# Two 64-column matmuls in place of one 128-column matmul, in the fp32 part of a linear-attention and mixer kernel

## The chip, the cores and the metric

One Trainium2 chip, one of its cores. The metric is device microseconds of one execution of the whole program. Of the kernel before there are three timed runs: 1278.36, 1279.97 and 1280.24 us, median 1279.97 us. One more execution was recorded by the hardware profiler.

## The reference

Random-feature attention over 8 batches, 8 heads, 576 tokens of 64 dimensions, then a token mixer and a two-layer MLP on the result. Cut to what matters:

```
phi(x): proj = x @ w_phi;  proj -= max|proj|;  return [exp(proj), exp(-proj)]      # 64 -> 2*128 features
kv  = phi(k).T @ v                  # per head 256 x 64, and z = sum of phi(k) over the tokens
out = phi(q) @ kv / (phi(q) @ z + 1e-6)
x   = heads side by side            # 8 x 576 x 512
u   = x + (x.T @ U @ V).T           # U 576 x 32, V 32 x 576
y   = u + relu(u @ w_ch1) @ w_ch2   # 512 -> 2048 -> 512
```

## The kernel before, in words

The work goes by **pairs** of heads: 8 batches with 4 pairs each. `Pair` loads k, q and v, transposes k and q on TensorE (`transposes`, L268), projects them with `w_phi` (`project_k`, `project_q`), makes the features (`k_features`, `q_features`; the maximum for q is a reduction over partitions on GpSimd, L327), and then has two steps that the change touches:

- *features with v*: `kv_tail` (L392) and `kv_main` (L400) add up `kv_ps`, 128 features x (64 values and one column of ones) for each half `f` of the 256 features and each of the two heads. The stationary operand is a 128 x 128 block of features (tokens x features), the moving one 65 columns of `vb`, or for the 64 left-over tokens of both heads ("tail") 130 columns of `vt`. `kv_done` (L407) copies the sum out of PSUM.
- *features with that product*: `out_tail` (L423) and `out_main` (L437) take 128 x 128 blocks of the q features as the stationary operand and 65 (tail: 130) columns of `kv` as the moving one. `normalize` divides.

All operands of these four are fp32. The program has one matmul for each; the hardware executes each fp32 one as two weight loads (LDWEIGHTS) and two matmuls, so that the profile counts 1024 for L403, where the program has 512, and as many for L442. Most other matmuls (the MLP at L559 and L576) use fp32r operands and are one load and one matmul each.

After the last pair of a batch, `Tokens` applies U and V (`down` L504, `up` L520) and the `Mixer` runs the MLP: `transposes` (L542) brings four token tiles into `uT_hi` and `uT_lo`, `hidden` (L553, 12 matmuls of 128x512) and `add` (L569, 12 more) run 16 times per batch. These MLP pieces are put into a list, and a hand-written loop (L724 to L757) calls a few of them between the steps of the next batch's pairs, so that TensorE has work while other engines make features. A ninth Mixer group holds the left-over tokens of all batches and runs last; its transposes stand at about 1170 us. In the first batch there is no MLP work yet; dummy matmuls (`keep_busy`, L655) fill some of the gaps.

What each engine does in which order is settled when the program is built: a scheduler with a timing model of its own orders the instructions of each engine by expected times, and each engine then runs its list strictly in that order. PSUM has three pools of banks: `at` (3 banks), `ph` (1), `o` (4). The last four hold the sum of the MLP's second layer from the first `add` of a batch to `finish` (L588), where VectorE adds them to `st`.

Of the kernel before, what the change touches and what calls it, by code (L numbers as in the profile page):

```python
# [18 lines left out]
PSUM = bass.MemoryType.PSUM  # L19
DRAM = bass.MemoryType.DRAM  # L20
P = 128


@with_exitstack
def tile_kernel(
# [12 lines left out]
    nc = tc.nc  # L38
    B, H, S, D = q.shape
    F = w_phi.shape[1]  # L40
# [5 lines left out]
        a.bitcast(I32).rearrange("a (b w) -> a b w", w=2) for a in (U, V, w1, w2))  # L46
    NT = S // P
    SM = NT * P
    ST = S - SM
    NPAIR = H // 2  # L50
    NCC = C // P
    NFC = DFF // P
    assert D == 64 and F == P and ST == 64 and 4 * R == P and B % 2 == 0

# [13 lines left out]
    def ps(name, tag="at"):  # L68
        return psum.tile([P, 512], F32, tag=tag, bufs=BANKS[tag], name=name)

# [158 lines left out]
    class Pair:  # L229
# [162 lines left out]
        def kv_tail(self):  # L392
            self.kv_ps = self.ps("kv_ps", True)
            self.kv_v = self.kv_ps[:, 0:4 * (D + 1)].rearrange("p (f h e) -> p f h e", f=2, h=2)
            for f in range(2):
                nc.tensor.matmul(  # L396
                    self.kv_v[:, f, :, :], self.kpt[:, 0, f * F:(f + 1) * F], self.vt,
                    start=(f == 0), stop=False, skip_group_check=True)

        def kv_main(self, g, kp):  # L400
            for t in range(NT):
                for f in range(2):
                    nc.tensor.matmul(  # L403
                        self.kv_v[:, f, g, :], kp[:, t, f * F:(f + 1) * F], self.vb[:, g, t, :],
                        start=False, stop=(t == NT - 1), skip_group_check=True)

        def kv_done(self):  # L407
            self.kv = small.tile([P, 2, 2, D + 1], F32, tag="kv", bufs=1, name=f"kv{self.nm}")
# [14 lines left out]
        def out_tail(self, xt):  # L423


            xp = self.ps("xpt", True)
            xv = xp[:, 0:2 * (D + 1)].rearrange("p (g e) -> p g e", e=D + 1)
            for f in range(2):
                nc.tensor.matmul(  # L429
                    xv, self.qpt[:, f, :], self.kv[:, f, :, :], start=(f == 0), stop=(f == 1))  # L430
            for g in range(2):
                rows = slice(g * ST, (g + 1) * ST)
                self.normalize(
                    f"t{g}", xv[rows, g:g + 1, :],
                    xt[self.tail, (self.h0 + g) * D:(self.h0 + g + 1) * D].unsqueeze(1), rows)

        def out_main(self, s, qp, x):  # L437
            xp = self.ps(f"xp{s}_", True)
            xv = xp[:, 0:NT * (D + 1)].rearrange("p (c e) -> p c e", e=D + 1)
            for c in range(NT):  # L440
                for f in range(2):
                    nc.tensor.matmul(  # L442
                        xv[:, c, :], qp[:, f, c * P:(c + 1) * P], self.kv[:, f, c // 2, :],
                        start=(f == 0), stop=(f == 1))
            xo = x.rearrange("p (z s) c -> p s z c", s=2)[:, s, :, self.h0 * D:(self.h0 + 2) * D]
            self.normalize(s, xv, xo.rearrange("p z (g d) -> p g z d", g=2))

# [350 lines left out]
```

## Time and profile before

| what | value |
|---|---|
| timed runs, median (lowest to highest) | 1279.97 us (1278.36 to 1280.24) |
| the profiled execution: span from first to last instruction | 1276.3 us |
| what lies around that span, if this execution took the median | 3.7 us |
| granted TensorE clock, mean | 0.994 |
| TensorE matmuls | 6976, busy 1244.0 us (97%) |
| TensorE weight loads | 6976, busy 1062.4 us (83%) |
| VectorE / ScalarE / GpSimd busy | 674.4 / 546.9 / 206.2 us |

The profile gives the execution's span and no other time of its own, so the third row is the difference to the median of the timed runs. In a profile, PE stands for TensorE's matmuls and PEld for its weight loads, which run beside them; DVE is VectorE, ACT ScalarE, POOL GpSimd. A row of a timeline is: start in us, length in us, engine, line of the kernel, operation, output<-inputs, size of the stationary operand (128\*128), output size, count. The length of a matmul there includes the time in the pipe and overlaps the next; what a matmul costs in a stream is the distance from its start to the next start.

### The profile page before, as it was taken

How to read it: one execution, taken by the hardware profiler on the slowest of the kernel's cores; microseconds unless marked ns; L12 is line 12 of the kernel's file. 1: busy time of each engine (PE TensorE's matmuls, PEld its weight loads, DVE VectorE, ACT ScalarE, POOL GpSimd, SP SyncE). 2: the span in 40 equal slices, each digit the busy share in tenths (PEclk: the TensorE clock that was granted, in tenths of full speed). 3: DMA queues.
4: the chain of work that ended last, by engine and by line, in shares of the span. 5: the costliest groups of instructions: out<-in, count | busy, mean ns of one | idle time of the engine just before them, and what ended most of it. 6: DMA issues, size and time to landing. Idle time of an engine off the chain costs nothing.

```text
span 1276.3 us, 18436 instructions
## 1 busy us (share of the span) xinstructions
PE 1244.0 (97%) x6976; PEld 1062.4 (83%) x6976; DVE 674.4 (53%) x1597; ACT 546.9 (43%) x1230; POOL 206.2 (16%) x184
## 2 busy tenths in 40 slices
PE   8999898999999999999999999999999999999997
PEld 6878677788888888888888888888888888788886
DVE  6579999755456455455545545545545542211211
ACT  6578777644443444344443444344434431111110
POOL 3335443301111111111110111011111110000000
PEclk9999998999999999999999999999999999999999
DMA  4245343421112111211112012211122002100001
GB/s 120 66 132 152 109 126 111 116 93 25 36 57 79 29 28 54 79 57 28 54 40 86 21 29 70 80 29 29 53 71 65 26 1 79 66 1 1 34 1 33
DMA packets 95159, 75.41 MB, mean 59 GB/s; under 512 B 52320, under 2 KB 77280, under 8 KB 94944
## 3 DMA queue, kind: packets, MB, share of 16 engines
q1 hardware_dynamic: 95072, 74.25, 19.4%
q8 instruction: 55, 0.90, 0.3%
q14 instruction: 32, 0.26, 0.1%
HBM read 55.35 MB, written 18.87 MB: 58 GB/s over the span
## 4 chain that ended last, share of the span: by engine, by line
PE 84%; DVE 11%; DMA 2%; ACT 1%; issue 1%; SPq 1%; POOL 0%; DVEq 0%; POOLq 0%
PE o L576 28%; PE ph L559 28%; PE xp L442 8%; PE kv_ps L403 7%; DVE w L141 2%; PE T L283 2%; PE pk L363 2%; DVE w_ab L149 1%; PE pp L514 1%; DMA w<-in_moe_w_ch_dram 1%; PE pt L546 1%; PE pq L386 1%; PE kv_ps L396 1%; PE xpt L429 1%; DVE w_ab L146 1%; PE pq L387 1%
## 5 line engine op out<-in xcount | busy, mean ns | idle before, releaser
L576 PE MATMUL o<-w_hi,h_hi 128*128 128x512 f32 x576 | 231.6, 404 | 1.3 <-ACT h_hi L564 0.9
L559 PE MATMUL ph<-uT_hi,w_hi 128*128 128x512 f32 x576 | 227.8, 396 | 1.8 <-ACT uT_hi L223 1.3
L559 PE MATMUL ph<-uT_lo,w_hi 128*128 128x512 f32 x576 | 227.8, 395 | 0.8 <-DVE uT_lo L224 0.8
L565 DVE SCALAR_TENSOR_TENSOR h_lo<-ph,h_hi 128x512 fp32r<-128x512 f32 x144 | 99.0, 687 | 243.7 <-ACT h_hi L564 242.0
L559 PE MATMUL ph<-uT_hi,w_lo 128*128 128x512 f32 x576 | 226.9, 394 | 0.5 <-DVE w_lo L211 0.5
L576 PE MATMUL o<-w_lo,h_hi 128*128 128x512 f32 x576 | 226.7, 394 | 0.0
L564 ACT ACTIVATE h_hi<-ph 128x512 fp32r<-128x512 f32 x144 | 85.8, 596 | 271.3 <-PE ph L559 261.8
L576 PE MATMUL o<-w_hi,h_lo 128*128 128x512 f32 x576 | 189.9, 396 | 0.0
L327 POOL PARTITION_ALL_REDUCE qp<-qp x64 | 125.6, 1963 | 355.2 <-ACT qp L326 311.8
L442 PEld LDWEIGHTS xp<-kv,qp 128*128 128x128 f32 x1024 | 124.4, 195 | 9.2 <-DVE kp L367 3.7
L442 PE MATMUL xp<-kv,qp 128*128 128x65 f32 x1024 | 126.1, 276 | 6.0 <-DVE kp L367 3.5
L576 PEld LDWEIGHTS o<-w_hi,h_hi 128*128 128x128 f32 x576 | 109.3, 190 | 23.8 <-ACT h_hi L564 2.8
L559 PEld LDWEIGHTS ph<-uT_hi,w_hi 128*128 128x128 f32 x576 | 108.5, 188 | 23.7 <-ACT uT_hi L223 1.9
L559 PEld LDWEIGHTS ph<-uT_lo,w_hi 128*128 128x128 f32 x576 | 108.4, 188 | 23.4 <-DVE uT_lo L224 2.3
L576 PEld LDWEIGHTS o<-w_lo,h_hi 128*128 128x128 f32 x576 | 109.3, 190 | 22.0 <-issue 0.8
L559 PEld LDWEIGHTS ph<-uT_hi,w_lo 128*128 128x128 f32 x576 | 108.5, 188 | 22.5 <-DVE w_lo L211 0.9
L403 PEld LDWEIGHTS kv_ps<-vb,kp 128*128 128x128 f32 x1024 | 122.8, 192 | 4.5 <-issue 1.4
L576 PEld LDWEIGHTS o<-w_hi,h_lo 128*128 128x128 f32 x576 | 106.5, 188 | 20.7 <-issue 0.2
L403 PE MATMUL kv_ps<-vb,kp 128*128 128x65 f32 x1024 | 122.2, 271 | 0.0
L266 DVE TENSOR_TENSOR T<-T,T 64x512 fp32r<-64x512 f32 x96 | 66.2, 689 | 94.0 <-ACT T L265 92.8
L265 ACT CAST T<-T 64x512 fp32r<-64x512 f32 x96 | 55.8, 582 | 96.4 <-PE pq L387 73.5
L327 POOL PARTITION_ALL_REDUCE qp_t<-qp_t x32 | 24.1, 754 | 375.3 <-ACT qp_t L326 375.3
(132 smaller groups left out, 1622.5 us busy)
## 6 DMA issues: line engine op xcount, KB each, us to landing
w<-in_moe_w_ch_dram SPq DMA_DIRECT2D x64, 256.0 KB, 3.0
raw<-in_k_dram SPq DMA_DIRECT2D x32, 256.0 KB, 2.8
raw<-in_q_dram SPq DMA_DIRECT2D x32, 256.0 KB, 2.9
vb<-in_v_dram SPq DMA_DIRECT2D x64, 128.0 KB, 2.6
u_dram<-x SPq DMA_DIRECT2D x32, 256.0 KB, 2.6
st<-u_dram SPq DMA_DIRECT2D x32, 256.0 KB, 3.8
out_dram<-st SPq DMA_DIRECT2D x32, 256.0 KB, 2.6
t_r<-in_k_dram SPq DMA_DIRECT2D x32, 32.0 KB, 2.1
```

Source lines behind the costliest of these rows:

```text
L141: nc.vector.tensor_scalar(out=halves[:, :, 0], in0=halves[:, :, 3], scalar1=0x7FF0, scalar2=None, op0=ALU.bitwise_and)
L265: nc.scalar.copy(out=dst[0:D], in_=src)
L266: nc.vector.tensor_sub(dst[D:2 * D], src, f32(dst[0:D]))
L283: nc.tensor.transpose(out=pT[:, c * P:(c + 1) * P], in_=self.raw[n][:, c // 2, c % 2, :], identity=ident)
L327: nc.gpsimd.partition_all_reduce(qp[:, 0, :], qp[:, 1, :], P, ReduceOp.absmax)
L363: nc.tensor.matmul(pk[:, i, :, :], self.T[0][:, i, cs], w_hl, start=True, stop=True)
L403: nc.tensor.matmul(self.kv_v[:, f, g, :], kp[:, t, f * F:(f + 1) * F], self.vb[:, g, t, :], start=False, stop=(t == NT - 1), skip_group_ch ...
L442: nc.tensor.matmul(xv[:, c, :], qp[:, f, c * P:(c + 1) * P], self.kv[:, f, c // 2, :], start=(f == 0), stop=(f == 1))
L559: nc.tensor.matmul(ph, l[:, c, fs], r[:, c, :], start=(n == 0), stop=(n == 3 * NCC - 1))
L564: nc.scalar.activation(out=h_hi, in_=ph, func=AF.Relu)
L565: nc.vector.scalar_tensor_tensor(out=h_lo, in0=ph, scalar=0.0, in1=f32(h_hi), op0=ALU.max, op1=ALU.subtract)
L576: nc.tensor.matmul(self.o[t], l[:, cs], r[:, f, :], start=(f == 0 and n == 0), stop=(f == NFC - 1 and n == 2))
```

## The change

Each of the four matmuls is replaced by two. The 128 stationary columns are cut into two halves of 64; the half `z` writes the partitions 64z to 64z+63 of the same PSUM bank, and the moving operand is the same for both. In the built program the two carry a tile of 128 rows x 64 columns of the array, one at column 0 and one at column 64; all others keep the 128 x 128 tile (but for 4 matmuls of L530, which had 64 columns and that tile already). Nothing is added up in another way.

```diff
+HP = 64
...
             for f in range(2):
-                nc.tensor.matmul(
-                    self.kv_v[:, f, :, :], self.kpt[:, 0, f * F:(f + 1) * F], self.vt,
-                    start=(f == 0), stop=False, skip_group_check=True)
+                for z in range(2):
+                    nc.tensor.matmul(
+                        self.kv_v[z * HP:(z + 1) * HP, f, :, :],
+                        self.kpt[:, 0, f * F + z * HP:f * F + (z + 1) * HP], self.vt,
+                        start=(f == 0), stop=False, skip_group_check=True)
...
                 for f in range(2):
-                    nc.tensor.matmul(
-                        self.kv_v[:, f, g, :], kp[:, t, f * F:(f + 1) * F], self.vb[:, g, t, :],
-                        start=False, stop=(t == NT - 1), skip_group_check=True)
+                    for z in range(2):
+                        nc.tensor.matmul(
+                            self.kv_v[z * HP:(z + 1) * HP, f, g, :],
+                            kp[:, t, f * F + z * HP:f * F + (z + 1) * HP], self.vb[:, g, t, :],
+                            start=False, stop=(t == NT - 1), skip_group_check=True)
...
-                nc.tensor.matmul(
-                    xv, self.qpt[:, f, :], self.kv[:, f, :, :], start=(f == 0), stop=(f == 1))
+                for z in range(2):
+                    zs = slice(z * HP, (z + 1) * HP)
+                    nc.tensor.matmul(
+                        xv[zs], self.qpt[:, f, zs], self.kv[:, f, :, :],
+                        start=(f == 0), stop=(f == 1), skip_group_check=True)
...
-                    nc.tensor.matmul(
-                        xv[:, c, :], qp[:, f, c * P:(c + 1) * P], self.kv[:, f, c // 2, :],
-                        start=(f == 0), stop=(f == 1))
+                    for z in range(2):
+                        zs = slice(z * HP, (z + 1) * HP)
+                        nc.tensor.matmul(
+                            xv[zs, c, :], qp[:, f, c * P + z * HP:c * P + (z + 1) * HP],
+                            self.kv[:, f, c // 2, :], start=(f == 0), stop=(f == 1),
+                            skip_group_check=True)
```

Because the scheduler orders by expected times, the order of other instructions moves as well. Three places follow; the line numbers of the changed kernel are higher by 1 to 11 than those before.

**TensorE, features with v, pair 1 of batch 4.** `kv_ps_1` is this pair's sum, `pq` the projection of its q (second half), `ph` an MLP matmul, `T` the transposes of the next pair. Before:

```order
L396 MATMUL kv_ps_1_5649<-vt_93,kp_1_t 128x130 x2
L403 MATMUL kv_ps_1_5649<-vb_94,kp_1_0_5469 128x65 x8
L386 MATMUL pq_4_1_5660<-T_4_1_5224,w_hl 128x512
L387 MATMUL pq_4_1_5660<-T_4_1_5224,w_hl 128x512
L403 MATMUL kv_ps_1_5649<-vb_94,kp_1_1_5509 128x65 x8
L559 MATMUL ph_3_5784<-uT_hi_5375,w_hi 128x512
```

After:

```order
L284 MATMUL T_4_2_6251<-ident,raw_2_1_6045 128x128 x4
L587 MATMUL o_3_6312<-w_hi,h_lo_1_6231 128x512
L398 MATMUL kv_ps_1_6261<-vt_93,kp_1_t 64x130 x4
L407 MATMUL kv_ps_1_6261<-vb_94,kp_1_0_6063 64x65 x16
L407 MATMUL kv_ps_1_6261<-vb_94,kp_1_1_6113 64x65 x16
L570 MATMUL ph_3_6424<-uT_hi_5969,w_hi 128x512
```

The counts double and the rows halve (64x65), the two halves of a block following each other. At this place `pq` has moved from between the two blocks to 12 MLP matmuls behind them.

**TensorE, the end of the attention part of batch 4 and the start of its MLP.** `vp_3` and `vp_4` are the last two products with V, `pt` the four transposes for the Mixer, `pkt` and `pk` projections of the next batch's pair 1, `ph_15` and `o` the MLP of the batch before, `ph_0` the first piece of the next. Before:

```order
L559 MATMUL ph_15_6672<-uT_hi_5375,w_lo 128x512
L546 MATMUL pt_0_6627<-ident,x_5448 128x128 x4
L530 MATMUL vp_4_6634<-pst_5892,v_all 64x512
L559 MATMUL ph_15_6672<-uT_hi_5375,w_hi 128x512
L559 MATMUL ph_15_6672<-uT_lo_5376,w_hi 128x512
L559 MATMUL ph_15_6672<-uT_hi_5375,w_lo 128x512
L576 MATMUL o_0_5679<-w_hi,h_lo_14_6622 128x512
L576 MATMUL o_1_5680<-w_hi,h_lo_14_6622 128x512
L576 MATMUL o_2_5681<-w_hi,h_lo_14_6622 128x512
L576 MATMUL o_3_5682<-w_hi,h_lo_14_6622 128x512
L546 MATMUL pt_1_6658<-ident,x_5448 128x128 x4
```

After:

```order
L587 MATMUL o_3_6312<-w_hi,h_lo_15_7424 128x512
L541 MATMUL vp_3_7301<-pst_6540,v_all 128x512
L557 MATMUL pt_0_7365<-ident,x_6042 128x128 x4
L541 MATMUL vp_4_7372<-pst_6540,v_all 64x512
L557 MATMUL pt_2_7403<-ident,x_6042 128x128 x4
L557 MATMUL pt_1_7396<-ident,x_6042 128x128 x4
L557 MATMUL pt_3_7427<-ident,x_6042 128x128 x4
L338 MATMUL pkt_1_7446<-w_hl,tail_T_1_7174 128x128
L339 MATMUL pkt_1_7446<-w_hl,tail_T_1_7174 128x128
L364 MATMUL pk_5_1_7456<-w_hl,T_5_1_7180 128x256 x2
L570 MATMUL ph_0_7592<-uT_hi_7363,w_hi 128x512
L364 MATMUL pk_5_1_7461<-w_hl,T_5_1_7180 128x256 x2
```

Before, the previous batch's MLP is still running between the transposes. After, it is finished ahead of `vp_3`, and no MLP matmul stands between `vp_3` and the next batch's `ph_0`. This form stands at the ends of batches 3, 4, 5 and 6.

**VectorE, the same place.** `x<-x,vp` adds the product with V, `st<-st,o` empties the four `o` banks, `uT_lo` is the low part of a transposed tile. Before:

```order
L531 TENSOR_TENSOR x_5448<-x_5448,vp_2_6559 128x512
L531 TENSOR_TENSOR x_5448<-x_5448,vp_3_6563 128x512
L531 TENSOR_TENSOR xt_5446<-xt_5446,vp_4_6634 64x512
L224 TENSOR_TENSOR uT_lo_6626<-pt_0_6627,uT_hi_6625 128x4x128
L565 SCALAR_TENSOR_TENSOR h_lo_15_6686<-ph_15_6672,h_hi_15_6685 128x512
L312 TENSOR_REDUCE mk_1_t<-pkt_1_6708 128x1
L224 TENSOR_TENSOR uT_lo_6626<-pt_1_6658,uT_hi_6625 128x4x128
```

After:

```order
L604 TENSOR_TENSOR st_0_7388<-st_0_7388,o_0_6309 128x512
L604 TENSOR_TENSOR st_1_7390<-st_1_7390,o_1_6310 128x512
L604 TENSOR_TENSOR st_2_7392<-st_2_7392,o_2_6311 128x512
L604 TENSOR_TENSOR st_3_7394<-st_3_7394,o_3_6312 128x512
L542 TENSOR_TENSOR x_6042<-x_6042,vp_3_7301 128x512
L542 TENSOR_TENSOR xt_6040<-xt_6040,vp_4_7372 64x512
L225 TENSOR_TENSOR uT_lo_7364<-pt_0_7365,uT_hi_7363 128x4x128
L225 TENSOR_TENSOR uT_lo_7364<-pt_2_7403,uT_hi_7363 128x4x128
L313 TENSOR_REDUCE mk_1_t<-pkt_1_7446 128x1
L225 TENSOR_TENSOR uT_lo_7364<-pt_1_7396,uT_hi_7363 128x4x128
L225 TENSOR_TENSOR uT_lo_7364<-pt_3_7427,uT_hi_7363 128x4x128
```

The four `st` additions now stand ahead of the addition for `vp_3` and of all four `uT_lo`.

## The prediction

> **What bounds the kernel now.** First the page's busy times and the chain that ended last, then the engines by stretches of the span.
>
> ```profile
> span 1276.3 us, 18436 instructions
> PE 1244.0 (97%) x6976; PEld 1062.4 (83%) x6976; DVE 674.4 (53%) x1597; ACT 546.9 (43%) x1230; POOL 206.2 (16%) x184
> PE 84%; DVE 11%; DMA 2%; ACT 1%; issue 1%; SPq 1%; POOL 0%; DVEq 0%; POOLq 0%
> ```
>
> ```profile
> 0.00:100.00 100.00, 92.80 (x614) 74.36 (x615) 67.23 (x195) 65.17 (x149) 32.54 (x43) 1.00 0.37 105
> 100.00:200.00 100.00, 92.15 (x506) 77.06 (x504) 96.72 (x246) 77.75 (x192) 47.27 (x53) 0.98 0.46 140
> 200.00:350.00 150.00, 142.01 (x793) 121.38 (x791) 97.68 (x233) 78.66 (x181) 32.02 (x28) 0.97 0.23 67
> 350.00:650.00 300.00, 299.33 (x1746) 260.93 (x1745) 159.63 (x373) 128.38 (x289) 39.67 (x26) 1.00 0.17 50
> ```
>
> The columns behind the length are PE, PEld, DVE, ACT, POOL. From 350 us on PE never stops (299.33 of 300), and no other engine is above 54% there. So each nanosecond of PE saved there comes off the end, until something else has to be waited for. In the first 200 us PE is at 92%, partly with dummies, DVE at 97% between 100 and 200: I credit nothing there.
>
> Next, what one of the touched matmuls costs. The weight loads of the middle of the program, and the matmuls around them:
>
> ```profile
> 702.28 0.64 PEld L396 LDWEIGHTS kv_ps<-vt,kp_t 128*128 128x128 f32 x4
> 702.84 1.87 PEld L403 LDWEIGHTS kv_ps<-vb,kp 128*128 128x128 f32 x16
> 704.62 0.19 PEld L386 LDWEIGHTS pq<-T,w_hl 128*128 128x128 f32 x1
> ```
> ```profile
> 702.50 0.61 PE L396 MATMUL kv_ps<-vt,kp_t 128*128 128x130 f32 x4
> 702.95 1.90 PE L403 MATMUL kv_ps<-vb,kp 128*128 128x65 f32 x16
> ```
>
> The 16 loads of L403 begin in 704.62 - 702.84 = 1.78 us: 111 ns each; I use 112 for load and matmul. The four tail matmuls of 130 columns take (702.95 - 702.50)/4 = 112 ns too: twice the columns, the same time. So 65 columns are not what takes it. A 256-column fp32 matmul shows what the streaming takes:
>
> ```profile
> 56.65 0.59 PE L348 MATMUL pk<-w_two,T 128*128 128x256 f32 x2
> 57.08 0.27 PE L274 MATMUL tT<-ident,t_r 128*128 128x128 f32 x1
> ```
>
> (57.08 - 56.65)/2 = 0.215 us for 256 columns, 0.84 ns per column: 55 ns for 65 and 109 ns for 130. So L403 and L442 are bound by the load of 128 columns (111), with 55 ns of streaming hidden under it, and the tails are bound by both. A load of 64 columns is in the trace too:
>
> ```profile
> L403 PEld LDWEIGHTS kv_ps<-vb,kp 128*128 128x128 f32 x1024 | 122.8, 192 | 4.5 <-issue 1.4
> L530 PEld LDWEIGHTS vp<-pst,v_all 128*64 128x64 f32 x4 | 0.5, 137 | 0.0
> ```
>
> 64 columns fewer make it 192 - 137 = 55 ns shorter. So a half is a load of about 55 ns and a stream of 55 ns.
>
> **The change part by part.**
>
> *The halves of L403 and L442.* Today 2048 x 112 ns = 229 us, of which from 200 us on:
>
> ```profile
> 200.00:1060.00 860.00, 90.93 (x768) 91.33 (x768) 0.99 0.17 52
> ```
> ```profile
> 200.00:1060.00 860.00, 98.08 (x800) 96.26 (x800) 0.99 0.17 52
> ```
>
> (the first for L403, the second for L442) 768 + 800 = 1568. After, there are two halves for each. No row of the trace shows two matmuls on different columns of the array, so the cost is bounded from both sides. Lower end: both halves load and stream at the same time, 55 ns for the two, 57 ns less than now. Upper end: one after the other with nothing overlapped, 55 + 55 for each half, 220 for the two, 108 ns more. In between lies strict turn-taking with each load under the stream before it, as the rows above show loads under streams: 55 to 57 ns for each half, 110 to 114 for the two, as now. I take the lower end: the halves write different partitions and use different columns, nothing in them is shared but what they read, and the trace shows the array already loading for one matmul while another streams. That gives 1568 x 57 = 89 us less. By the Trainium skill, "TensorEngine Tiling (Array Packing)", Key Properties, tiles are independent and can load and multiply in parallel; no run here shows it.
>
> Of that, each unbroken run of halves gives back a step of 55 ns, since its first and last half have no partner. The order of the changed kernel has 156 such runs, about 130 of them behind 200 us: 130 x 55 ns = 7 us back. Saved: 82 us.
>
> *The tails.* 256 x 112 = 29 us now. Their stream of 109 ns is the bound; side by side two halves take 110 ns, as one does now: 0. In turns they take 2 x 110: 28 us more.
>
> *The moved order.* `pq` behind 12 MLP matmuls (first place of the order) feeds ACT, POOL and DVE and is used by `xp` some 60 rows later, behind MLP matmuls: 0, and if that cover were gone, about one POOL reduction (1963 ns). The second and third place cost something. Rows for these:
>
> ```profile
> L327 POOL PARTITION_ALL_REDUCE qp<-qp x64 | 125.6, 1963 | 355.2 <-ACT qp L326 311.8
> ```
> ```profile
> L224 DVE TENSOR_TENSOR uT_lo<-pt,uT_hi 128x512 fp32r<-128x512 f32 x36 | 24.1, 683 | 15.2 <-ACT uT_hi L223 14.8
> L531 DVE TENSOR_TENSOR x<-x,vp 128x512 f32<-128x512 f32 x32 | 21.5, 684 | 21.8 <-PE vp L530 21.7
> L593 DVE TENSOR_TENSOR st<-st,o 128x512 f32<-128x512 f32 x32 | 20.3, 680 | 5.0 <-PE o L576 5.0
> L312 DVE TENSOR_REDUCE mk_t<-pkt 128x1 f32<-128x128 f32 x32 | 9.1, 285 | 20.6 <-PE pkt L338 15.4 <-PE pkt L340 5.2
> ```
>
> Between the last `o` matmul and the first matmul of `ph_0` that reads `uT_lo`, DVE now has 4 x 0.68 (`st`) + 2 x 0.68 (`x`, `xt`) + 4 x 0.68 (`uT_lo`) + 0.3 (`mk_t`) = 7.1 us in a row. It can begin some 0.7 us ahead of that last `o` matmul, three matmuls earlier. PE has two `vp` and one `ph` (0.23 us each, the distance of 512 columns in the rows below), 16 transposes (about 0.11 each, there too), and `pkt` and four `pk` of half the columns (0.65 together): 3.1 us. It waits 7.1 - 0.7 - 3.1 = 3.3 us, at the end of four batches: 13 us, taken as 14 with the hops between engines. Queued behind the waiting `ph_0` is everything on PE. Ends: 0 (if DVE gets there earlier) and 25.
>
> *Switching between tiles of 128 and 64 columns.* 312 switches after. The trace has four, and the same sequence without one:
>
> ```profile
> 954.34 0.60 PE L546 MATMUL pt<-ident,x 128*128 128x128 f32 x4
> 954.70 0.48 PE L530 MATMUL vp<-pst,v_all 128*64 128x512 f32 x1
> 955.01 0.39 PE L559 MATMUL ph<-uT_hi,w_hi 128*128 128x512 f32 x1
> 955.24 0.39 PE L559 MATMUL ph<-uT_lo,w_hi 128*128 128x512 f32 x1
> ```
> ```profile
> 1172.17 0.60 PE L546 MATMUL pt<-ident,x_tail 128*128 128x128 f32 x4
> 1172.52 0.48 PE L559 MATMUL ph<-uT_hi,w_hi 128*128 128x512 f32 x1
> 1172.83 0.40 PE L559 MATMUL ph<-uT_lo,w_hi 128*128 128x512 f32 x1
> ```
>
> From the first transpose to the second matmul behind: 0.67 us with the 64-column tile, 0.66 without. At most 10 ns, 312 times: 0 to 3 us; I take 0.
>
> Sum against the profiled execution: 1276.3 - 82 + 0 + 14 = 1208.3 us of span; with the 3.7 us to the median of the runs, **1212 us**. Its own range: if the first 200 us gain as well (480 x 57 = 27 us) and DVE costs nothing, 1171; if only half the gain is had because loads keep up less well, 1253.
>
> **The rivals.**
>
> *Loads take turns, streams don't matter* (A). If only one load runs at a time, two halves load in 2 x 55 = 110 ns: no gain. For it: the load is the bound now and nothing shows two at once. Against: different columns. Time: 0 + 14 for the moved order, 1280 + 14 = 1294; by its ends (two halves in 108 to 116 ns, 8 us either way, and DVE's 0 to 25) between 1272 and 1313.
>
> *Everything takes turns* (B). Then the halves stream one after the other as well. A stream that equals its load costs a little over either (112 instead of 109 for the tails), so 58 ns per half with the same 3 ns, 63 as an upper end: 4096 x 58 to 63 = 238 to 258 instead of 229, 9 to 29 us; the tails 28; the order 14. 1331 to 1351. For it: every matmul in the trace starts after the one before it by its load or its stream.
>
> *A load waits for the stream before it* (C). 110 ns per half: 4096 x 110 = 451 instead of 229, +222; tails 512 x (55 + 109) = 84 instead of 29, +55; order +14: 1571. It decides as soon as the tile's load can't start until its own rows are free. By the Trainium skill, "TensorE: Matmul & The Clock Gate", Part 3, a load overlaps matmuls under way only in other rows of the array, and these halves use all the same rows. The trace speaks against it for whole tiles and after a 64-column one:
>
> ```profile
> 954.67 0.14 PEld L530 LDWEIGHTS vp<-pst,v_all 128*64 128x64 f32 x1
> 954.78 0.19 PEld L559 LDWEIGHTS ph<-uT_hi,w_hi 128*128 128x128 f32 x1
> ```
>
> the load at 954.78 lies within the matmul that began at 954.70 and runs 0.48 us.
>
> *Each switch empties the array* (D). Side by side as forecast, but each of the 312 switches pays what the pipe hides, a matmul's length less the distance to the next:
>
> ```profile
> L403 PE MATMUL kv_ps<-vb,kp 128*128 128x65 f32 x1024 | 122.2, 271 | 0.0
> ```
>
> 271 - 112 = 159 ns, 50 us. 1212 + 50 = 1262. The four switches above show none of it. By the Trainium skill, "TensorEngine Tiling (Array Packing)", Key Properties, a change of tiling mode drains the engine; the trace, with at most 10 ns, does not bear that out.
>
> *It doesn't do what it says.* The built program carries both column positions, so this has no chance of its own; halves that share one position in the end are B.
>
> **How the numbers follow.** Chances: forecast 0.50, A 0.16, B 0.21, C 0.08, D 0.05. About 0.2%, 2.6 us, is what a measurement of this kernel tells from no change. Faster: the forecast, D and the part of A in which DVE costs little, 0.50 + 0.05 + 0.03 = 0.58. Same: 0.05, from A. Slower: the rest of A, B and C, 0.08 + 0.21 + 0.08 = 0.37. The range must leave out at most 2 in 10: C (0.08) and the upper part of B go; from 1171, with a few us for the unknown start, 1165, to 1335. The forecast's own range is 1171 to 1253.
>
> **What would show it.** In the changed profile: PEld rows of 64 columns beginning two by two, 16 blocks of a former 1.78 us now 32 halves in about 0.9 us (A and B: 1.8 to 2.0; C: 3.5); tail halves 4 to 0.22 us (B: 0.44); PE waits for `uT_lo` of about 3 us at four places; the matmul behind a run of halves starting no later than 0.32 us after the run's last (D: 0.16 more). The forecast is wrong if 32 halves still take 1.7 us or more, or if PE, now faster, waits for POOL or ACT in every pair.

## The result and the profile after

The changed kernel takes 1243.09 us (median of 4 runs, 1241.68 to 1244.36); the kernel before took 1279.64 in the same runs (1278.36 to 1280.24). The ratio is 0.9709, 95% interval 0.9695 to 0.9724: faster by 36.6 us. The forecast was 1212, so about half of the gain that it counted on came.

The head of the profile after, the busy times and the shares of the chain that ended last:

```profile
span 1239.6 us, 23026 instructions
PE 1189.8 (96%) x9267; PEld 959.5 (77%) x9280; DVE 672.5 (54%) x1597; ACT 545.8 (44%) x1230; POOL 208.0 (17%) x184
PE 81%; DVE 13%; DMA 2%; ACT 1%; issue 1%; POOL 0%; SPq 0%; DVEq 0%; POOLq 0%
```

PE is still the bound, with 54 us less of busy time; DVE's share of the chain went from 11 to 13%. The loads of the halves and their matmuls, grouped by line (busy us, then mean ns of one):

```profile
L452 PEld LDWEIGHTS xp<-kv,qp 128*64 128x64 f32 x2048 | 68.6, 140 | 21.9 <-issue 4.4 <-DVE kp L368 3.3 <-ACT w_hi L218 2.8
L407 PEld LDWEIGHTS kv_ps<-vb,kp 128*64 128x64 f32 x2048 | 67.8, 138 | 13.5 <-issue 11.7 <-ACT kp_t L318 0.4 <-DMA w<-in_moe_w_ch_dram 0.4
```

Twice the loads of before in 67.8 us, where half as many took 122.8. How that comes about shows in one block of 16 former matmuls, PE and then the weight loads (start, length):

```profile
699.18 1.09 PE L587 MATMUL o<-w_hi,h_lo 128*128 128x512 f32 x4
700.20 1.15 PE L452 MATMUL xp<-kv,qp 128*64 128x65 f32 x32
701.28 0.50 PE L364 MATMUL pk<-w_hl,T 128*128 128x256 f32 x2
```
```profile
699.42 0.41 PEld L587 LDWEIGHTS o<-w_hi,h_lo 128*128 128x128 f32 x2
700.20 1.01 PEld L452 LDWEIGHTS xp<-kv,qp 128*64 128x64 f32 x32 [0.36 <-DVE den_t L421]
701.28 0.30 PEld L364 LDWEIGHTS pk<-w_hl,T 128*128 128x128 f32 x2
```

The 32 loads end 1.01 us after the first began; less the last one's 0.14 that is 0.87 us for 15 steps from pair to pair, 58 ns a pair. A pair does what one matmul did in 112, so 54 ns are saved on each. But look at the ends. No load is under way between the end of those at 699.42 (699.83) and 700.20, and the load of `pk` begins only at 701.28, together with its matmul. Before, the load behind a block began under the block's streams (704.62, while the matmuls of L403 ran from 702.95 to 704.85). I took the distances of starts from both traces, medians over blocks between matmuls of 512 columns:

| distance, ns | before | after |
|---|---|---|
| last matmul ahead to the block's first | 226 | 318 |
| first of the block to last | 1618 | 932 |
| last of the block to the matmul behind | 83 | 150 |
| from there to the next | 315 | 337 |
| together | 2242 | 1737 |

A block gains 505 ns, where 16 x 54 = 864 were to be had. The missing 359 ns belong to its two ends. The three steps there are 181 ns longer, and the second pair starts 102 to 108 behind the first and not 58, some 50 more. The rest is that the block's first and last step had less to give: by starts they took some 56 and 83 ns before, not 112. A tail that stands alone has only ends, and loses as much: from the matmul ahead to the one behind it is 590 ns before and 927 after, and 22 more to the next. (The row of `xp` names DVE's `den_t` for its pause; for L407 the profile names nothing, `issue`, for 11.7 of 13.5 us.)

Where along the span the gain comes is seen from one mark in both programs, the copy of `kv` for the first pair of heads of each batch (L409, now L414):

| batch | 1 | 2 | 3 | 4 | 5 | 6 | 7 | end |
|---|---|---|---|---|---|---|---|---|
| before, us | 84.5 | 247.8 | 385.4 | 524.7 | 664.7 | 804.1 | 944.1 | 1276.3 |
| after, us | 85.4 | 247.1 | 383.3 | 516.8 | 650.5 | 783.8 | 917.5 | 1239.6 |
| earlier by | -0.9 | 0.7 | 2.1 | 7.9 | 14.0 | 20.3 | 26.6 | 36.7 |
| MLP matmuls (`ph` and `o`) run by then, more than before | 0 | -4 | 21 | 22 | 22 | 22 | 22 | 0 |

By the mark alone nothing comes until 383 us. But PE's order moved as well: by that mark the changed kernel has run 21 MLP matmuls more than the kernel before by its own (730 and 709). At 0.23 us each that is 4.9 us, so at 383 us it leads by 7 us and not by 2. Counted so, nothing comes until 247 us, then 7 us in that batch and 6.0 to 6.3 in each of the next four, of 139.7 us. The engines by stretches (PE, PEld, DVE, ACT, POOL):

```profile
200.00:350.00 150.00, 138.22 (x1110) 111.15 (x1109) 101.69 (x244) 81.16 (x187) 34.91 (x31) 0.99 0.24 74
350.00:650.00 300.00, 296.42 (x2482) 244.42 (x2480) 162.92 (x380) 133.31 (x299) 39.68 (x26) 1.00 0.18 52
```

Between 200 and 350 us PE was busy for 142.01 us before and is for 138.22 now, and has run 23 MLP matmuls more in that time (389 and 366). From 350 us on it now pauses, 3.6 us in 300. At a batch's end that looks so (PE):

```profile
794.11 0.60 PE L557 MATMUL pt<-ident,x 128*128 128x128 f32 x4
795.86 1.09 PE L557 MATMUL pt<-ident,x 128*128 128x128 f32 x8 [1.15 <-DVE x L542]
...
797.31 0.50 PE L364 MATMUL pk<-w_hl,T 128*128 128x256 f32 x2 [0.18 <-DVE uT_lo L225]
797.68 0.50 PE L570 MATMUL ph<-uT_hi,w_hi 128*128 128x512 f32 x1
798.79 0.47 PE L364 MATMUL pk<-w_hl,T 128*128 128x256 f32 x2 [0.61 <-DVE uT_lo L225]
799.29 0.50 PE L570 MATMUL ph<-uT_lo,w_hi 128*128 128x512 f32 x1
```

From the last full-length `vp` (793.21) to `ph` with `uT_lo` (799.29) 6.1 us pass for 3.1 us of matmuls: 3.0 us of waiting. The same place before had some of it as well:

```profile
823.52 0.49 PE L363 MATMUL pk<-w_hl,T 128*128 128x256 f32 x2
824.44 0.50 PE L559 MATMUL ph<-uT_hi,w_hi 128*128 128x512 f32 x1 [0.43 <-ACT uT_hi L223]
825.17 0.50 PE L559 MATMUL ph<-uT_lo,w_hi 128*128 128x512 f32 x1 [0.22 <-DVE uT_lo L224]
```

`pk` to `ph` 0.92 us where two `pk` take 0.24, `ph` to `ph` 0.73 where 0.23 is usual: 1.2 us. But of the five ends behind 383 us only two were like this. At the other three `ph` with `uT_lo` came 0.37 us behind `pk`:

```profile
684.47 0.39 PE L363 MATMUL pk<-w_hl,T 128*128 128x256 f32 x2
684.84 0.50 PE L559 MATMUL ph<-uT_lo,w_hi 128*128 128x512 f32 x1
```

By the starts at all five, PE waits 13.8 us after (2.5 to 3.0 at each) and 2.8 before. The change added 11 us, 2.2 a batch.

### The profile page after: what moved, and what is told of

It reads as the page before. It is cut to its first block, busy times and chain, and to the rows that moved or that the text cites. A ratio compares the mean times of both kernels' runs of the same rounds, so it can differ in the third digit from the quotient of the medians.

```text
span 1239.6 us, 23026 instructions
## 1 busy us (share of the span) xinstructions
PE 1189.8 (96%) x9267; PEld 959.5 (77%) x9280; DVE 672.5 (54%) x1597; ACT 545.8 (44%) x1230; POOL 208.0 (17%) x184
## 4 chain that ended last, share of the span: by engine, by line
PE 81%; DVE 13%; DMA 2%; ACT 1%; issue 1%; POOL 0%; SPq 0%; DVEq 0%; POOLq 0%
PE ph L570 29%; PE o L587 29%; PE xp L452 5%; PE kv_ps L407 4%; PE T L284 2%; PE pk L364 2%; DVE w L142 2%; DMA w<-in_moe_w_ch_dram 2%; DVE w_ab L150 2%; PE pp L525 1%; PE pq L387 1%; PE kv_ps L398 1%; PE xpt L436 1%; DVE uT_lo L225 1%; DVE st L604 1%
## 5 line engine op out<-in xcount | busy, mean ns | idle before, releaser
L587 PE MATMUL o<-w_hi,h_lo 128*128 128x512 f32 x576 | 192.6, 395 | 0.0
L452 PEld LDWEIGHTS xp<-kv,qp 128*64 128x64 f32 x2048 | 68.6, 140 | 21.9 <-issue 4.4
L452 PE MATMUL xp<-kv,qp 128*64 128x65 f32 x2048 | 76.8, 227 | 8.6 <-DVE kp L368 3.0
L266 ACT CAST T<-T 64x512 fp32r<-64x512 f32 x96 | 55.7, 580 | 53.8 <-PE pq L388 34.5
L407 PEld LDWEIGHTS kv_ps<-vb,kp 128*64 128x64 f32 x2048 | 67.8, 138 | 13.5 <-issue 11.7
L367 ACT COPY kp<-pk 128x256 f32<-128x256 f32 x96 | 35.3, 370 | 97.3 <-PE pk L364 97.2
```

What stands on the lines that cost most here:

```text
L266: nc.scalar.copy(out=dst[0:D], in_=src)
L367: nc.scalar.copy(out=kp[:, ts_, 0:F], in_=pk[:, :, 1, :])
L407: nc.tensor.matmul(self.kv_v[z * HP:(z + 1) * HP, f, g, :], kp[:, t, f * F + z * HP:f * F + (z + 1) * HP], self.vb[:, g, t, :], start=Fals ...
L452: nc.tensor.matmul(xv[zs, c, :], qp[:, f, c * P + z * HP:c * P + (z + 1) * HP], self.kv[:, f, c // 2, :], start=(f == 0), stop=(f == 1), s ...
L587: nc.tensor.matmul(self.o[t], l[:, cs], r[:, f, :], start=(f == 0 and n == 0), stop=(f == NFC - 1 and n == 2))
```

## The experiments

The theory after the comparison (theory 1): side by side works as forecast, and each change between tiles of 64 and 128 columns costs PE 0.16 to 0.18 us (about half of the 359 ns, since a block has two), because no load is taken under the stream ahead of it and the next stream starts behind that load. The rival (theory 2): changes are free, and the gain fell short for the moved order, at the batches' ends above all. All times are medians of 4 runs; the ratios, with their 95% intervals, are to runs of the kernel before on the same chip.

**More changes of tile, nothing else.** One matmul of a constant in the middle of each block, 128 in all, its output read by nobody; once it fills the array, once it is a half (`ident_bf16` stands for the identity's bits read as bf16):

```
             for t in range(NT):
+                if t == NT // 2:
+                    matmul(self.kv_ps[:, 320:384], ident_bf16[:, 0:128], ident_bf16[:, 0:64])
+                #   the half:   (self.kv_ps[0:64, 320:384], ident_bf16[:, 0:64], ident_bf16[:, 0:64])
                 for f in range(2):
```
(and the same in `out_main`.)

> The changed kernel with one bf16 matmul of 128 stationary columns and 64 moving columns put in the middle of each of the 128 blocks (64 of features with v, 64 of features with that product); it writes a corner of the bank that nothing reads. Changes between 64- and 128-column tiles: 566 in place of 312. Theory 1 (each change of tile size costs TensorE 0.16 to 0.18 us): 254 x 0.16 to 0.18 = 41 to 46 us over the changed kernel's 1243, plus 128 x 0.00 to 0.06 us for the matmuls themselves: 1284 to 1297 us. Theory 2 (changes of tile are free; the gain fell short because work moved at the batches' ends and because a block's first load stands alone): 1243 to 1251 us.

> The same with the extra matmul of 64 stationary columns instead of 128 (column tile 0, bf16, 64 moving columns): 318 changes of tile in place of 312, so it prices the extra matmul without the change of tile. Both theories: 1243 plus 128 x 0.00 to 0.06 us, 1243 to 1252 us. What tells them apart is the kernel with 128 columns less this one: theory 1 248 x 0.16 to 0.18 = 40 to 45 us, theory 2 0 to 4 us.

Measured: 1268.20 us (0.9914, 0.9899 to 0.9928) and 1247.33 us (0.9745, 0.9729 to 0.9762). The difference is 20.9 us, half of what theory 1 expected, and far from theory 2. The two blocks in the timeline of PE, first with the 128-column one, then with the half:

```profile
623.30 0.69 PE L411 MATMUL kv_ps<-vb,kp 128*64 128x65 f32 x16
623.92 0.20 PE L406 MATMUL kv_ps<-ident 128*128 128x64 bf16 x1
624.05 0.69 PE L411 MATMUL kv_ps<-vb,kp 128*64 128x65 f32 x16
```
```profile
627.18 0.64 PE L462 MATMUL xp<-kv,qp 128*64 128x65 f32 x16
627.65 0.19 PE L456 MATMUL xp<-ident 128*64 128x64 bf16 x1
627.66 0.68 PE L462 MATMUL xp<-kv,qp 128*64 128x65 f32 x16
```

From half to half across the inserted one: 0.75 us for 16 halves and the 128-column one, 0.48 for 16 and the 64-column one. By the starts of single matmuls, the four pairs around it take 466 ns against 232. So 234 ns go to two changes and the matmul, 117 or less for each change. Why the sum was smaller: I had counted all 128 blocks. By the copy of `kv` the two kernels draw apart by 14.4 us in four batches, 225 ns for each of 64 blocks, but by only 1.5 us in the 383 us ahead of them: 3.6 us in the 16 blocks from 247 us on, 225 ns each again, while at 247 us the kernel with the 128-column one was 2.1 us the earlier, for a reason that no run shows. The mechanism held, its size and its place did not. Half of the 359 ns was too much for a change: 231 of them, the longer steps and the second pair, are what 2 x 117 can explain, and the short first and last step are the rest.

**Fewer changes.** Both blocks of features with v behind one another, both of the product behind one another, the tail last:

```
 def s_kv0_q1: kv_tail, kv_main(0)
-    project_q(1)                  # moved to s_kv1
+    kv_main(1), kv_done
...
-step(cur.s_out0, x, xt)           # tail, then block 0; s_out1 followed a step later
+cur.s_out0(x)
+cur.s_out1(x)
+step(cur.out_tail, xt)            # its first matmul keeps its place in the program's order
...
```

> The changed kernel with its halves in longer runs: both blocks of features with v behind one another, both blocks of features with the product behind one another and the tail's four behind those. 212 changes of tile in place of 312, same matmuls. Theory 1: 100 x 0.16 to 0.18 = 16 to 18 us below the changed kernel, 1225 to 1227, and 2 to 4 either way for the moved order at the batches' ends: 1221 to 1231 us. Theory 2: no gain from longer runs, 1238 to 1248 us.

Measured: 1225.38 us (0.9579, 0.9565 to 0.9594), 17.7 below the changed kernel. That fits theory 1, but its order also shortens the wait at a batch's end: the largest there is now 0.7 us, on ACT's `uT_hi`, with another of 0.65 for DVE's `uT_lo` at two of the five ends. So the order was measured alone, with whole matmuls:

> The kernel before, whole matmuls, with the order of the kernel with longer runs (both blocks of features with v behind one another, both blocks of the product and then the tail behind one another): no change of tile is added or saved, so it prices the moved order alone, of which the kernel with longer runs (1225, 18 below the changed kernel) has its share. Theory 1: 1274 to 1281 us, from 1280 less up to 6 us for the shorter waits at the batches' ends, so that 12 to 18 us of the 18 belong to the 50 runs fewer. Theory 2: the whole 18 us come from the order, 1262 us.

Measured: 1286.84 us (1.0070, 1.0053 to 1.0087). This was outside of both expectations: the order costs 8.6 us where nothing changes tile. By the copy of `kv` it loses 6.7 us before 385 us, 6.0 of them before 248, and 0.4 in each batch behind. So the gain of the longer runs is not a gain of their order. In the steady batches they are 3.8 us faster than the changed kernel. The trace has 9 runs of halves in a batch there instead of 16; 7 x 0.36 is 2.5, and about 1 comes from shorter waits at the batch's end (some 1.8 us instead of 2.8, the mean of five ends).

**What a change costs, and between which tiles.** The kernel before, with one extra matmul of 64 columns in the middle of each block, in column tile 0, in column tile 64, in another type, and two of them:

```
+                if t == NT // 2:
+                    matmul(self.kv_ps[0:64, 320:384], ident_bf16[:, 0:64], ident_bf16[:, 0:64])
+                #   column tile 64: self.kv_ps[64:128, 320:384]
+                #   float32r:       w_hl[:, 0, 0:64] as both operands
+                #   two:            the first line twice
```

> The kernel before (whole matmuls of 128 stationary columns) with one bf16 matmul of 64 stationary columns, column tile 0, in the middle of each of the 128 blocks, written to an unread corner of the bank: 264 changes of tile in place of 8, none of which involves column tile 64. Theory 1 (any change between 128 and 64 columns is paid, 0.11 to 0.13 us each as the two kernels with extra matmuls gave it, 96 of the 128 blocks after the first 250 us): 96 x 2 x 0.11 to 0.13 = 21 to 25 us, 1280 + that = 1301 to 1305. Theory 1b (only changes to or from a pair of column tiles, or to column tile 64, are paid; the four 64-column matmuls of the kernel before showed none): 1280 plus up to 96 x 0.06 = 1280 to 1286. Theory 2 (free): the same as 1b.

> The same with the extra matmul in column tile 64 (it writes partitions 64 to 127). Theory 1 and theory 1b: 1301 to 1305 us. Theory 2: 1280 to 1286 us. If this one is paid and the one in column tile 0 is not, the price belongs to column tile 64 and not to the size.

> The kernel before with the extra 64-column matmul of column tile 0 as before, but in float32r in place of bf16; size and place of the tile are the same. If every change of size is paid whatever the type: 96 blocks x 0.30 us as for bf16 = 28 to 37 us, 1306 to 1316 us. If a 64-column float32r matmul keeps the array in the mode of the 128-column ones (which would be why the four of the kernel before showed no price): its own time alone, 96 x 0.03 to 0.11 us, 1281 to 1289 us.

> The kernel before with two extra bf16 matmuls of column tile 0 behind one another in the middle of each block, where the earlier run had one: the same 264 changes of tile, twice the extra matmuls. If the price is the change: 1315 + 96 to 128 x 0.03 to 0.06 = 1318 to 1323 us, and half of what remains of 289 ns is the price of a change, 115 to 130 ns. If the price is the matmul's own: 36 us more again, 1351 us.

Measured: column tile 0 1314.60 us (1.0282, 1.0267 to 1.0297), column tile 64 1314.66 (1.0284, 1.0268 to 1.0299), float32r 1289.14 (1.0083, 1.0068 to 1.0099), two of column tile 0 1311.74 (1.0260, 1.0245 to 1.0275). The weight loads of one block each, bf16, then float32r, then two:

```profile
601.77 0.97 PEld L454 LDWEIGHTS xp<-kv,qp 128*128 128x128 f32 x8
602.81 0.11 PEld L449 LDWEIGHTS <-ident 128*64 128x64 bf16 x1
602.96 0.97 PEld L454 LDWEIGHTS xp<-kv,qp 128*128 128x128 f32 x8
603.85 0.19 PEld L590 LDWEIGHTS o<-w_hi,h_hi 128*128 128x128 f32 x1
```
```profile
603.88 0.97 PEld L408 LDWEIGHTS kv_ps<-vb,kp 128*128 128x128 f32 x8
604.77 0.14 PEld L403 LDWEIGHTS kv_ps<-w_hl 128*64 128x64 f32 x1
604.83 0.97 PEld L408 LDWEIGHTS kv_ps<-vb,kp 128*128 128x128 f32 x8
605.73 0.19 PEld L386 LDWEIGHTS pq<-T,w_hl 128*128 128x128 f32 x1
```
```profile
612.15 0.97 PEld L412 LDWEIGHTS kv_ps<-vb,kp 128*128 128x128 f32 x8
613.19 0.11 PEld L403 LDWEIGHTS <-ident 128*64 128x64 bf16 x1
613.22 0.11 PEld L407 LDWEIGHTS <-ident 128*64 128x64 bf16 x1
613.37 0.97 PEld L412 LDWEIGHTS kv_ps<-vb,kp 128*128 128x128 f32 x8
614.26 0.19 PEld L386 LDWEIGHTS pq<-T,w_hl 128*128 128x128 f32 x1
```

From the block's first load to the load behind it: 1.78 us in the kernel before, 2.08 with one bf16 matmul, 1.85 with the float32r one, 2.11 with two. The second of the two costs 0.03 us. What the first costs beyond that, by single starts 289 - 32 = 257 ns, is the price of two changes: 128 ns each, the same into column tile 0 as into 64. Theory 1 holds, 1b and theory 2 fall. (That the inserted matmul is bf16 and its neighbours fp32 is not what is paid: the 64-column bf16 one among halves cost 0.03 us.) The float32r matmul has the same tile and pays nothing but its 0.06 to 0.08 us: its load starts 0.11 us behind the one ahead, as loads in a row do, while the bf16 one leaves 0.26 us. By the Trainium skill, "PSUM — Partial Sum Buffer", The four PSUM rules, a float32r matmul always carries the mask of all column strips; then it would be no change at all, which these rows agree with without showing the mask. (The totals missed what theory 1 had said, 1301 to 1305 us for one and 1318 to 1323 for two, and don't follow the order of their blocks. In the steady batches they lose 4.75 and 5.2 us per batch, as they should. The rest lies ahead of 248 us, where the kernel with one is 8.7 us late and the kernel with two 3.1; why is not shown.)

**The columns take turns.** The loops turned, so that neighbours share a column tile:

```
-for t ...: for f ...: for z in range(2):
+for z in range(2): for t ...: for f ...:
```

> The changed kernel with the loops turned: of each block first all halves of column tile 0, then all of column tile 64, so that neighbours share a column tile but once per block. Same matmuls, same 312 changes of tile. If the gain comes from two column tiles that load and stream at the same time, a half now takes its load of 55 ns or more alone, 32 halves 1.8 us in place of 0.93: 96 blocks after the first 250 us x 0.85 = 82 us over 1243, 1310 to 1335 us. If halves overlap however they are ordered: 1240 to 1250 us. In the trace, the step into a run is then one into column tile 0 and the step out one from column tile 64: about 92 and 67 ns over the kernel before's if a change of size is paid whichever the tile.

Measured: 1320.55 us (1.0323, 1.0297 to 1.0348), as expected of taking turns. A block of the product, PE:

```profile
372.68 1.85 PE L452 MATMUL xp<-kv,qp 128*64 128x65 f32 x32
374.46 0.50 PE L364 MATMUL pk<-w_hl,T 128*128 128x256 f32 x2
```

32 halves of which neighbours share columns need 1.78 us to the next matmul, about what 16 whole ones took before (1618 + 83 ns); side by side it is 1.08. So the gain is that two column tiles load and stream at the same time, and only neighbours in the queue do. The step into such a run (column tile 0) is 318 ns and out of it (column tile 64) 150, as in the changed kernel.

**Better versions.** The runs joined further, across the pairs of heads, and two kernels that tell why that failed and where the longer runs still lose:

```
# joined, on top of the longer runs (not shown: q's tail projection and MLP pieces move too)
 cur.s_out0(x)
 cur.s_out1(x)
-step(cur.out_tail, xt)
+cur.out_tail(xt)
+nxt.s_kv0_q1()                    # the next pair's tail and both blocks
-tag, bufs = ("feat", 3) if ng > 1 else ("feat_t", 2)
+tag, bufs = ("feat", 4) if ng > 1 else ("feat_t", 2)
-NW = 8
+NW = 6
# longer runs with six wide buffers: NW = 6 alone
# late: the longer runs' order for a pair of heads only where
+self.grouped = b >= 2
```

> Longer runs still: the blocks of features with the product of one pair of heads and the tail's are followed at once by the next pair's two blocks of features with v, 72 or 56 halves that only the work for which the scheduler finds room parts. 182 changes of tile in place of 312. To hold the features longer it has one buffer more for them and six in place of eight for the wide tiles. Theory 1: 130 x 0.16 to 0.18 = 21 to 23 us below the changed kernel, 1220 to 1222, up to 15 us more where the six buffers or the moved order make TensorE wait: 1220 to 1237 us. Theory 2: 1240 to 1260 us.

> The kernel with longer runs (1225) with six wide buffers in place of eight, as the joined one had (1245). If the missing buffers took the joined kernel's gain: 1240 to 1250 us. If its order did (TensorE's waits for VectorE at the batches' ends): 1224 to 1230 us.

> The longer runs from the third batch on only; the first two batches keep the changed kernel's order, since the whole matmuls in that order lost their 6.7 us in the first 350 us. 228 changes of tile in place of 312 (and 212). If that loss is one of the order in the first two batches: 1225 less 2 to 5, 1220 to 1224 us. If it was a matter of the whole matmuls alone: 1224 to 1228 us.

Measured: joined 1244.95 us (0.9732, 0.9718 to 0.9747), no gain, and in the range of theory 2: fewer runs alone don't give the time; the longer runs with six buffers 1229.88 (0.9620, 0.9606 to 0.9635); late 1220.51 (0.9549, 0.9533 to 0.9565). The buffers cost some 5 us. The other 15 go with the joined order, whose largest PE waits between 350 and 1000 us are these (us in all, times, longest):

```profile
PE pt L560 <- DVE x L545: 6.8, 5, 1.4
PE vp L544 <- DVE T L267: 5.3, 5, 1.1
```

So 182 changes there bought nothing against 212. I read these waits as ends of batches where nothing is left to lay over DVE's chain, which no run tests alone. (It also has one buffer more for the features, which was not tried alone.) The late version is the best of all, 22.6 us below the changed kernel. In the steady stretch its PE is fuller than there, and just as full as with the longer runs throughout (297.57 of 300 us too); the 5 us that it gains on those it has by its mark at 376 us, where theirs is at 382:

```profile
350.00:650.00 300.00, 297.57 (x2517) 248.70 (x2516) 169.41 (x388) 138.25 (x301) 41.87 (x27) 1.00 0.19 54
```

## Why the prediction was right in sign and too low

*Halves side by side: right.* 58 ns a pair where 55 was taken, and the turned loops, with the same matmuls and as many changes, take the gain away. A, B and C fall: 32 halves take 0.93 us, not 1.7 or more. Three ns a pair are 1568 x 3 = 5 us of the sum.

*Switching between tiles: the step that failed.* It said "At most 10 ns, 312 times: 0 to 3 us; I take 0." The four rows it rested on were float32r matmuls, which pay nothing with 64 columns. The halves are plain fp32 and pay. A change cost 117 ns between halves and a 128-column bf16 matmul and 128 between whole matmuls and a 64-column one; a run of halves among the MLP's matmuls paid 359 ns, its two changes and its short first and last step. D's 159 a change was near, but D had a chance of 0.05 on the strength of a row of another type. By the Trainium skill, "TensorEngine Tiling (Array Packing)", Key Properties, a change of tiling mode drains the engine; with 117 to 128 ns for bf16 and fp32 the runs now agree that it costs time, and the float32r rows are where they do not. The sign that I named for D, the matmul behind a run starting more than 0.32 us after the run's last, would have missed it: it starts after 0.15. The price is spread over the step into the run (92 ns more than before), the second pair (about 50), the step out (67) and the one behind (22).

*The runs: fewer, and dearer.* It gave back 130 x 55 ns = 7 us for halves without a partner. The trace has 100 runs behind 200 us, and with their changes they cost 100 x 359 ns = 36 us.

*Where the credit begins: nearly right.* Of the 98 blocks credited from 200 us on, the 4 ahead of 247 us brought nothing; they were some 3 us of the sum. (The mark alone would say that 20 blocks brought 2 us together; the MLP matmuls run by then say otherwise.)

*The waits at the batches' ends: right in kind, too large.* 2.5 to 3.0 us are waited at each where 3.3 was said, in the order of DVE's work that was named, at five ends and not four. But 0.1 or 1.2 of it was there before, so the change added 11 us instead of 14.

*Tails and `pq`: 0, as said.* In a run of 40 the tail's halves go at 110 ns a pair; where a tail stands alone, 8 halves, it loses about 0.36 us at its two ends, as counted above. No wait of PE's for POOL's reduction shows.

The sum again with these sizes, from 247 us on, where the trace has 94 blocks and 96 runs: 94 x 864 ns = -81.2; 96 x 359 ns = +34.5; the waits +11. That makes -35.7 us against 36.7 measured. The prediction had -89, +7 with 0 for the changes, and +14: of the 31 us of span that it missed, 27 are in the ends of the runs. (The 3.7 us that it put around the span were 2.1 in this execution, 1241.68 less 1239.6.) The 359 ns are read from the same trace, so this shows that nothing large is left over; the price of a change itself rests on the inserted matmuls.

That the time still lies within what was forecast is in part luck. The range was held open up to 1253 us for loads that keep up less well and to 1335 for taking turns, and neither is what happened.

## What to carry to other kernels

A load-bound fp32 matmul with a short stream gains almost a factor of two from two column tiles (here 112 to 58 ns), if halves of different columns are neighbours in the queue. Count the runs, not only the matmuls: each run of halves between full matmuls paid about 0.23 to 0.36 us here, so a run must hold five to seven former matmuls (5 x 54 = 270, 7 x 54 = 378 ns) to pay, and putting blocks behind one another was worth another 1.4 to 1.8%. Take the price of a mode from a row of the same type. And read a gain along the span by a mark and by the work done up to it: here the mark alone was off by 5 us.

## What the runs showed that was not expected

- A change between 64- and 128-column tiles costs 117 to 128 ns in plain bf16 and fp32, the same for both column tiles; a 64-column float32r matmul among 128-column ones costs its own 0.06 to 0.08 us and no change.
- A second small matmul behind a change is nearly free, 0.03 us; and a 64-column bf16 one among halves (1247.33 against 1243.09 us for 128 of them) costs 0.03 us.
- The order of PE's work ahead of 250 us alone moves the end by several us: the whole matmuls in the order of the longer runs are 6.0 us late at 248 us. So sizes were read by batch behind it.
